# Attention stages given to a scheduler 150 places earlier than the expert steps around them

## The chip, the cores and the metric

The kernel runs on one core of a Trainium2 chip. The metric is the device time of the whole program in microseconds (us). A core has five engines that run their own instruction queues side by side and meet only at semaphores: PE (TensorE, matmuls), DVE (VectorE), ACT (ScalarE), POOL (GpSimd) and SP (SyncE, which here only issues DMAs). Each queue is served in order: an instruction that waits holds everything behind it on its engine.

## The reference

Three layers follow each other, all in fp32. Attention has 4 batches of 8 heads, 576 positions, 64 wide, and each position sees the last 64. The heads are put side by side to 2304 tokens x 512. Expert layer 1 takes 512 to 2048 and back, expert layer 2 takes 512 to 1024 and back.

```python
# attention, q k v: (4, 8, 576, 64)
scores = scale * np.matmul(q, k.transpose(0, 1, 3, 2))
mask = (rel >= 0) & (rel < window)            # rel = query position - key position, window = 64
attn = np.exp(scores - max);  attn = attn / (np.sum(attn) + 1e-09)
x = (attn @ v).transpose(0, 2, 1, 3).reshape(2304, 512)
# layer 1
h = x @ w_in                                  # 512 -> 2048
g = np.where(h >= 1, h, np.where(h <= -1, 0.0, (h + 1) ** 2 / 4))
x = g @ w_out                                 # 2048 -> 512
# layer 2
h = x @ w_in2                                 # 512 -> 1024
solu = h * softmax(h)
x = (layer_norm(solu) * g_ln) @ w_out2        # 1024 -> 512
```

## The kernel before

**Numbers.** Each fp32 factor of an expert matmul is split into a high and a low part, and a product is three matmuls (high-high, high-low, low-high). So each weight tile is converted before its first use: after its DMA (L124 for w_in, L126 for w_out, 512 KB each, five landing buffers `wst`) ACT rescales it (L132), DVE shifts and merges bits (L136, L137), ACT casts the high part (L145), and DVE subtracts to get the low part (L146). `wih`, `wil` are the parts of w_in, `woh`, `wol` those of w_out. There are 16 tiles of each, one per slice f of 128 hidden features.

**Layer 1.** Tokens go in six blocks j of 384, with the 16 slices f inside. A unit of work is one (j, f): 12 matmuls for h (L496), ACT relu and square (L505, L506), DVE min/max (L511, writes `u`), ACT cast (L512), a subtraction for the low part (L516, on POOL in block 0, then on DVE), and, two units later in the program's order, 12 matmuls that add the unit into the output (L527). The weights are loaded and converted during block 0 and stay on chip, so the later blocks need none. The first two slices of block 0 are done in halves of 192 tokens.

**Attention between the units.** Attention goes by groups g (one tile of 192 tokens, two heads), in pairs P of groups from g = 18. A group has loads of q and k (`load_qk`, eight DMAs of 24 or 32 KB, L291, into five `qk` buffers), DVE transposes into `kq` (L325, L326, or L317 for pairs), scores on PE (L352, or L442 for pairs), masked maxima on DVE (L360, L452), exps on ACT (L366, L458), a division on DVE (L377, L378, L382, L386; POOL divides the first three tiles), transposes of the probabilities on PE (L402), copies of these on ACT (L407), probabilities times v on PE (L421, L476), and the result's high part on ACT and low part on DVE (L428, L429, L483, L484), which are `xh` and `xl`, the inputs of layer 1. The function `slots()` is a generator that yields after each stage: four stages a group, eight a pair. The main loop calls `slot(n0)` after the unit's h and before its min/max, and `slot(n1)` after the output matmuls of two units earlier, so two stages fall into each unit (more in the half units).

**What sets the order.** The program runs under a tile framework whose scheduler takes the instructions in the order of their priority, which is the order in which the Python code gives them unless the code says otherwise, and simulates the engines to place each of them in its engine's queue. A stage's loads on SP are ordered the same way as its matmuls.

Of the kernel before, what the change touches and what calls it, by code (L numbers as in the profile page):

```python
# [20 lines left out]
def kernel(  # L21
# [579 lines left out]
    def slots():  # L601
        for g in range(G0 + 1, GB + 1):
            st_s(g)
            yield
            st_v(g - 1)
            st_norm(g)
            yield
            qkt_and_loads(g + 1)
            v_ahead(g)
            yield  # L610
            st_t(g)
            if g == GB:
                st_s(g + 1)
            yield
        st_norm(GB + 1)
        qkt_and_loads(2 * PU)
        yield
        st_v(GB)
        st_t(GB + 1)
        qkt_and_loads(2 * PU + 1)  # L620
        yield
        for P in range(PU, NPP + 1):
            if P == PU:
                st_v(GB + 1)
            else:
                pair_v(P - 1)
            if P % NPR == 0:
                v_ahead(2 * P)
            if P < NPP:
                pair_s(P)  # L630
            yield
            if P < NPP:
                st_norm(P, 0)
                st_norm(P, 1)
            yield
            qkt_and_loads(2 * P + 2)
            yield
            qkt_and_loads(2 * P + 3)
            yield
            yield  # L640
            yield
            if P < NPP:
                st_t(P, 0)
                st_t(P, 1)
            yield
            yield

    stages = slots()

    def slot(n):  # L650
        for _ in range(n):
            next(stages, None)

    TPN = NB // 128
    NK2 = DF2 // 128
# [192 lines left out]
    for n in range(len(seq) + 2):  # L848
# [29 lines left out]
        if n < len(seq):  # L878
            prev = part
            slot(n0)  # L880
            w_conv()
            pins = moe_g2(*part)
# [5 lines left out]
        if n < len(seq):  # L888
            slot(n1)
            w_conv()  # L890
            if j == 0:
                w_load(2)
            w2_step(n, *pins)
            if last and f < 2:
                w2_vals(f)
            if last and f in (2, 3):
                w2_sums(f - 2)
            if last and f >= 2:
                with tc.issue_after(pins[0]):
                    w2_split(f - 2)  # L900
            if last and 2 <= f < 10:
                w2_load(f - 2)
        else:
            w_conv()
# [82 lines left out]
```

## Time and profile before

| | before |
|---|---|
| median of three runs | 707.45 us (706.28, 707.45, 707.75) |
| profiled execution: time | 705.73 us |
| profiled execution: span | 704.0 us |
| mean granted TensorE clock | 0.995 of 2.4 GHz |
| PE busy | 681.7 us, 97% |
| DVE busy | 442.6 us, 63% |
| ACT busy | 411.8 us, 58% |
| POOL busy | 147.6 us, 21% |

The span runs from the first to the last instruction that the profiler saw; the execution's time is 1.7 us more. A busy share is an average over stages that have different limits: in block 0 of layer 1 (about 61 to 141 us) the weights are loaded and converted, in blocks 1 to 5 they are not. An end that is followed by idle time in brackets, as in "[0.76 <-DVE u L511]", says that the engine stood still for 0.76 us before that instruction and that the last thing to arrive was the DVE's result `u` of line 511.

### The profile page before, as it was taken

What the parts mean: (1) busy time and instruction counts of PE and PEld (TensorE: products, weight loads), DVE (VectorE), ACT (ScalarE), POOL (GpSimd) and SP (SyncE); (2) the same over time, 40 slices, a digit from 0 to 9 for tenths busy, and PEclk for the clock granted to TensorE, in tenths of its full rate; (3) what the DMA queues carried; (4) which work ended last, traced back from release to release, by engine and by line L of the source; (5) the groups of instructions that cost most, each with busy time, mean ns of one, the idle gap of its engine ahead of it and who ended that gap; (6) DMA issues with size and microseconds to landing.
All of it is one profiled execution on the core that took longest, in us unless ns stands there. A gap on an engine that the chain in (4) does not pass through costs nothing.

```text
span 704.0 us, 12616 instructions
## 1 busy us (share of the span) xinstructions
PE 681.7 (97%) x4439; PEld 627.7 (89%) x4439; DVE 442.6 (63%) x1179; ACT 411.8 (58%) x1006; POOL 147.6 (21%) x185
## 2 busy tenths in 40 slices
PE   6889999899999999999999999999999999999998
PEld 5689888799999999999999999999987788888887
DVE  4669998556455555454455553642379999988850
ACT  5779777565556655565566565354454746345451
POOL 2313222200001000021112111652272322220000
PEclk9989999999999999999999999999999999999999
DMA  9996798534354524346352211562024465534321
GB/s 188 206 277 179 191 245 215 121 62 108 72 115 106 119 65 77 75 129 125 86 113 67 99 48 43 173 200 92 1 102 123 150 194 166 183 131 141 127 93 46
DMA packets 155543, 88.94 MB, mean 126 GB/s; under 512 B 118616, under 2 KB 141400, under 8 KB 155480
## 3 DMA queue, kind: packets, MB, share of 16 engines
q1 hardware_dynamic: 144040, 64.00, 36.9%
q0 software_dynamic: 8704, 19.41, 8.4%
q10 hardware_dynamic: 2736, 4.72, 1.8%
q8 instruction: 35, 0.57, 0.4%
q14 instruction: 28, 0.23, 0.1%
HBM read 63.97 MB, written 24.12 MB: 125 GB/s over the span
## 4 chain that ended last, share of the span: by engine, by line
PE 74%; DVE 9%; issue 6%; ACT 5%; DMA 4%; POOL 2%; SPq 1%; DVEq 0%; POOLq 0%; ACTq 0%
PE ps_h L496 22%; PE acc L527 22%; PE ps_o L826 13%; PE P L711 8%; DMA wst<-in_moe_w_in_dram 2%; PE ps_x L476 2%; POOL wil L249 2%; PE ps_p L402 2%; PE ps_s L442 2%; PE ps_s L352 1%; ACT p L366 1%; DVE wst L137 1%; DVE gl L516 1%; PE ps_x L421 1%; DVE s L740 1%
## 5 line engine op out<-in xcount | busy, mean ns | idle before, releaser
L511 DVE SCALAR_TENSOR_TENSOR u<-u,ps_h 128x384 f32<-128x384 f32 (+1 forms) x98 | 53.2, 543 | 140.2 <-ACT u L506 139.2
L496 PE MATMUL ps_h<-xh,wih 128*128 128x384 f32 (+1 forms) x392 | 132.1, 338 | 3.1 <-DVE u L511 2.1
L496 PE MATMUL ps_h<-xl,wih 128*128 128x384 f32 (+1 forms) x392 | 131.5, 336 | 0.6 <-DVE xl L429 0.5
L527 PE MATMUL acc<-gl,woh 128*128 128x384 f32 (+1 forms) x392 | 130.5, 334 | 1.5 <-DVE gl L516 1.3
L496 PE MATMUL ps_h<-xh,wil 128*128 128x384 f32 (+1 forms) x392 | 131.4, 335 | 0.0
L527 PE MATMUL acc<-gh,wol 128*128 128x384 f32 (+1 forms) x392 | 129.5, 333 | 0.0
L527 PE MATMUL acc<-gh,woh 128*128 128x384 f32 (+1 forms) x392 | 128.5, 342 | 0.5 <-ACT gh L512 0.5
L505 ACT ACTIVATE u<-ps_h,half 128x384 f32<-128x384 f32 (+1 forms) x98 | 56.0, 572 | 92.7 <-PE ps_h L496 92.5
L512 ACT CAST gh<-u 128x384 fp32r<-128x384 f32 (+1 forms) x98 | 49.7, 507 | 54.6 <-DVE u L511 37.4
L496 PEld LDWEIGHTS ps_h<-xh,wih 128*128 128x128 f32 x392 | 74.3, 190 | 4.9 <-DVE u L511 3.3
L527 PEld LDWEIGHTS acc<-gh,woh 128*128 128x128 f32 x392 | 72.7, 189 | 3.8 <-issue 2.6
L527 PEld LDWEIGHTS acc<-gl,woh 128*128 128x128 f32 x392 | 73.7, 188 | 2.6 <-DVE gl L516 1.7
L516 DVE TENSOR_TENSOR gl<-u,gh 128x384 fp32r<-128x384 f32 x80 | 52.4, 655 | 37.2 <-ACT gh L512 36.7
L496 PEld LDWEIGHTS ps_h<-xl,wih 128*128 128x128 f32 x392 | 74.5, 190 | 1.2 <-DVE xl L429 0.9
L496 PEld LDWEIGHTS ps_h<-xh,wil 128*128 128x128 f32 x392 | 74.6, 190 | 0.1
L527 PEld LDWEIGHTS acc<-gh,wol 128*128 128x128 f32 x392 | 73.6, 188 | 0.1
L711 PE MATMUL P<-wih,x2p 128*128 128x512 f32 x216 | 70.8, 391 | 1.4 <-DVE xo L539 0.9
L826 PE MATMUL ps_o<-woh,wol 128*128 128x512 f32 (+1 forms) x152 | 57.7, 380 | 0.3 <-DVE wol L814 0.3
L826 PE MATMUL ps_o<-woh,woh 128*128 128x512 f32 (+1 forms) x152 | 57.7, 379 | 0.0
L826 PE MATMUL ps_o<-wol,woh 128*128 128x512 f32 (+1 forms) x152 | 57.5, 378 | 0.0
L506 ACT ACTIVATE u<-u 128x384 f32<-128x384 f32 (+1 forms) x98 | 51.1, 522 | 1.9
L711 PEld LDWEIGHTS P<-wih,x2p 128*128 128x128 f32 x216 | 40.4, 188 | 10.4 <-DVE xo L539 1.3
(125 smaller groups left out, 1208.8 us busy)
## 6 DMA issues: line engine op xcount, KB each, us to landing
vw<-in_v_dram SPq DMA_DIRECT2D x32, 256.0 KB, 5.1
wst<-in_moe_w_in_dram SPq DMA_DIRECT2D x16, 512.0 KB, 5.8
wst<-in_moe_w_out_dram SPq DMA_DIRECT2D x16, 512.0 KB, 4.7
lnd<-e SPq DMA_DIRECT2D x16, 512.0 KB, 2.8
lT<-lnd SPq DMA_DIRECT2D x64, 128.0 KB, 2.9
x2d<-xo POOLq DMA_DIRECT2D x24, 192.0 KB, 2.5
out_dram<-o ACTq DMA_DIRECT2D x17, 256.0 KB, 2.0
wst<-in_moe_w_in_dram POOLq DMA_DIRECT2D x8, 512.0 KB, 5.5
```

The source lines that it names most:

```text
L249: nc.gpsimd.tensor_tensor(lo, v_, as_f32(hi), op=ALU.subtract)
L402: nc.tensor.transpose(ps[:, i * 128:i * 128 + 128], p[:, i, :], ident)
L442: nc.tensor.matmul(ps[x][64 * c:64 * c + 64, i * 128 + c0:i * 128 + 128], z[r, KQ + i * 64:KQ + i * 64 + 64], z[r, i * 64 + c0:i * 64 + 12 ...
L496: nc.tensor.matmul(ps, a, bb[:, kc, c], start=(n == 0), stop=(n == 3 * KC - 1))
L505: nc.scalar.activation(u, ps, ACTF.Relu, bias=half, scale=0.5)
L506: nc.scalar.activation(u, u, ACTF.Square)
L511: g = nc.vector.scalar_tensor_tensor(u, u, 1.0, ps, op0=ALU.min, op1=ALU.max)
L512: return nc.scalar.copy(hi, u).ins, g.ins
L516: eng.tensor_tensor(lo, u, as_f32(hi), op=ALU.subtract)
L527: nc.tensor.matmul(acc[j, e][:, c], a, bb, start=(f == 0 and n == 0 and c.start == 0), stop=(f == NF - 1 and n == 2),)
L711: nc.tensor.matmul(ps, l, r, start=(n == 0), stop=(n == 5))
L826: nc.tensor.matmul(ps, a[kk // 4][:, kk % 4, :], b[kk][:, c:c + w], start=(n == 0), stop=(n == 3 * NK2 - 1),)
```

## The change

The stage call is put into a context that gives every instruction of the stage, its DMA issues too, a priority 150 instructions further up. Nothing is added or removed, and every engine has the same instructions as before. After this edit lines from 653 on carry numbers one higher.

```diff
     def slot(n):
         for _ in range(n):
-            next(stages, None)
+            with tc.high_priority(150):
+                next(stages, None)
```

On SP's queue the place is the middle of block 0, where the weights of slice f = 8 follow those of f = 7. `wst` are weights, and each `qk` row is a run of loads for attention groups 13, 14 and so on. Before:

```order
L124 DMA wst<-in_moe_w_in_dram 128x4x256
L126 DMA wst<-in_moe_w_out_dram 128x1024
L291 DMA qk<-in_q_dram 32x6x32 x3
L124 DMA wst<-in_moe_w_in_dram 128x4x256
L291 DMA qk<-in_q_dram 32x6x32
L291 DMA qk<-in_k_dram 32x6x32 x4
L291 DMA qk<-in_q_dram 32x6x32 x4
L126 DMA wst<-in_moe_w_out_dram 128x1024
```

And now, where the first two rows are again the weights of f = 7 and the next `wst` row is w_in of f = 8:

```order
L124 DMA wst<-in_moe_w_in_dram 128x4x256
L126 DMA wst<-in_moe_w_out_dram 128x1024
L291 DMA qk<-in_q_dram 32x6x32 x4
L291 DMA qk<-in_k_dram 32x6x32 x4
L291 DMA qk<-in_q_dram 32x6x32 x4
L291 DMA qk<-in_k_dram 32x6x32 x4
L291 DMA qk<-in_q_dram 32x6x32 x4
L291 DMA qk<-in_k_dram 32x6x32 x4
L124 DMA wst<-in_moe_w_in_dram 128x4x256
L291 DMA qk<-in_q_dram 32x6x32 x4
L291 DMA qk<-in_k_dram 32x8x32 x4
L126 DMA wst<-in_moe_w_out_dram 128x1024
```

The load of w_in for f = 8 stands behind three q/k loads before and behind 24 now, and that of w_out for f = 8 behind 12 before and 32 now. At f = 15, the last slice, w_in stands behind 48 before and 72 now, counted from group 13 on.

On DVE the place is the conversion of the same tile, w_in of f = 8 (`wil_792` is its low part, `wol_788` the low part of w_out for f = 7). Before:

```order
L146 TENSOR_TENSOR wol_788<-wst,woh_787 128x512
L360 ISA p,mx<-ps_s,mask 128x128
...
L325 STREAM_TRANSPOSE kq_125<-qk 64x3x64 x2
L326 STREAM_TRANSPOSE kq_125<-qk 128x192
L511 SCALAR_TENSOR_TENSOR u<-u,ps_h 128x384
L136 TENSOR_SCALAR wst<-wst 128x512
L146 TENSOR_TENSOR wil_792<-wst,wih_791 128x512
```

And now, where the L136 is the shift of w_in for f = 8 itself:

```order
L146 TENSOR_TENSOR wol_788<-wst,woh_787 128x512
L377 TENSOR_SCALAR sm<-sm 128x3
L378 RECIPROCAL rs<-sm 128x3
L511 SCALAR_TENSOR_TENSOR u<-u,ps_h 128x384
L429 TENSOR_TENSOR xl<-ps_x,xh 128x192
L136 TENSOR_SCALAR wst<-wst 128x512
L137 SCALAR_TENSOR_TENSOR wst<-wst 128x512
L511 SCALAR_TENSOR_TENSOR u<-u,ps_h 128x384
...
L325 STREAM_TRANSPOSE kq_124<-qk 64x3x64 x2
L326 STREAM_TRANSPOSE kq_124<-qk 128x192
L146 TENSOR_TENSOR wil_792<-wst,wih_791 128x512
```

The tile's low part stands two units of work ahead of the matmuls that use it before (eight L511 rows precede it in the block), and directly ahead of them now (ten do). From the shift of f = 8 to the low part of w_in for f = 15, DVE's queue now holds, beyond what stood between the low parts of f = 8 and f = 15 before: two L136, one L137, one L146, six maxima with their reads (L360), one L317, two L325, one L326, two L377, one L378, two L382, two L386 and two L429.

On PE the place is a unit of block 1, at the transposes of a pair's probabilities (L402). Before:

```order
L496 MATMUL ps_h<-xh,wih_494 128x384
L496 MATMUL ps_h<-xl,wih_494 128x384
L496 MATMUL ps_h<-xh,wil_495 128x384
L402 MATMUL ps_p<-ident,p 128x128 x6
```

And now:

```order
L527 MATMUL acc_2050<-gh,wol_173 128x384
L496 MATMUL ps_h<-xh,wih_494 128x384
L402 MATMUL ps_p<-ident,p 128x128 x6
L496 MATMUL ps_h<-xl,wih_494 128x384
L496 MATMUL ps_h<-xh,wil_495 128x384
```

The stage follows the first of a unit's 12 matmuls instead of the last: 11 matmuls earlier, and so for each stage of blocks 1 to 4. In block 0 the stages come up to 85 matmuls earlier. When PE reaches the first L442, both orders have the same work behind them, and in the last 1319 rows of PE nothing differs. From the last low part of w_in (f = 15) to the first L442, PE now has 66 matmuls of 384 columns, two groups of L402, one of L352 and two of L421.

## Rows read from the trace of the kernel before

**Rows 1.** The page: busy time of each engine and its share of the span.
```profile
PE 681.7 (97%) x4439; PEld 627.7 (89%) x4439; DVE 442.6 (63%) x1179; ACT 411.8 (58%) x1006; POOL 147.6 (21%) x185
```

**Rows 2.** Windows: stretch, length, busy PE PEld DVE ACT POOL, clock, DMA share, GB/s.
```profile
80.00:100.00 20.00, 18.90 (x119) 17.52 (x119) 19.05 (x43) 15.89 (x36) 5.36 (x5) 1.00 0.85 213
100.00:120.00 20.00, 19.22 (x129) 17.82 (x128) 17.81 (x49) 16.19 (x43) 5.75 (x6) 1.00 0.98 239
120.00:141.00 21.00, 18.78 (x140) 16.76 (x138) 12.76 (x46) 11.73 (x39) 5.95 (x8) 1.00 0.51 113
...
250.00:300.00 50.00, 50.00 (x408) 48.47 (x407) 26.32 (x88) 30.56 (x83) 4.22 (x8) 1.00 0.35 74
```

**Rows 3.** Timeline of PE: start, us, instruction, count, idle before and its releaser.
```profile
82.35 0.33 PE L496 MATMUL ps_h<-xh,wih 128*128 128x384 f32 x1
...
119.70 0.44 PE L496 MATMUL ps_h<-xh,wih 128*128 128x384 f32 x1 [0.76 <-DVE u L511]
...
133.58 0.52 PE L402 MATMUL ps_p<-ident,p 128*128 128x128 f32 x3 [1.37 <-DVE p L386]
...
135.58 0.44 PE L496 MATMUL ps_h<-xh,wih 128*128 128x384 f32 x1 [0.81 <-DVE mx L360]
...
141.45 0.78 PE L442 MATMUL ps_s<-kq 64*64 64x128 f32 x20
```

**Rows 4.** Timeline of SP's DMA issues: start, us for the run, instruction, count.
```profile
63.50 1.30 SPq L291 DMA_DIRECT2D qk<-in_q_dram  x3
64.91 0.39 SPq L124 DMA_DIRECT2D wst<-in_moe_w_in_dram  x1
65.34 0.51 SPq L291 DMA_DIRECT2D qk<-in_q_dram  x1
...
71.28 0.39 SPq L126 DMA_DIRECT2D wst<-in_moe_w_out_dram  x1
...
120.50 1.92 SPq L291 DMA_DIRECT2D qk<-in_k_dram  x4
```

**Rows 5.** The page's DMA issues: count, KB each, median us to landing.
```profile
wst<-in_moe_w_in_dram SPq DMA_DIRECT2D x16, 512.0 KB, 5.8
```

**Rows 6.** Timeline of DVE: low parts of w_in for f = 8 and 15.
```profile
77.12 0.68 DVE L146 TENSOR_TENSOR wil<-wst,wih 128x512 fp32r<-128x512 f32 x1
...
118.53 0.65 DVE L146 TENSOR_TENSOR wil<-wst,wih 128x512 fp32r<-128x512 f32 x1
119.10 0.54 DVE L511 SCALAR_TENSOR_TENSOR u<-u,ps_h 128x384 f32<-128x384 f32 x1
```

**Rows 7.** DVE by line, 77.8 to 119.2 us: busy, mean ns, idle before.
```profile
L137 DVE SCALAR_TENSOR_TENSOR wst<-wst 128x512 uint32<-128x512 uint32 x15 | 11.0, 734 | 0.3 <-ACT wst L132 0.3
L136 DVE TENSOR_SCALAR wst<-wst 128x512 uint32<-128x512 uint32 x14 | 8.2, 584 | 2.9 <-DMA wst<-in_moe_w_in_dram 1.7 <-DMA wst<-in_moe_w_out_dram 1.2
L146 DVE TENSOR_TENSOR wil<-wst,wih 128x512 fp32r<-128x512 f32 x8 | 5.4, 672 | 0.0
L146 DVE TENSOR_TENSOR wol<-wst,woh 128x512 fp32r<-128x512 f32 x7 | 4.8, 682 | 0.8 <-ACT woh L145 0.8
...
L325 DVE STREAM_TRANSPOSE kq<-qk 64x192 f32<-64x192 f32 x6 | 2.2, 368 | 0.1
L360 DVE CUSTOM_DVE_ANT_0 p<-ps_s,mask 128x128 f32<-128x128 f32 (+1 forms) x9 | 1.9, 259 | 0.0
L377 DVE TENSOR_SCALAR sm<-sm 128x3 f32<-128x3 f32 x3 | 1.3, 435 | 0.0
...
L429 DVE TENSOR_TENSOR xl<-ps_x,xh 128x192 fp32r<-128x192 f32 x3 | 1.0, 346 | 0.0
L386 DVE TENSOR_TENSOR p<-p,rs 128x256 f32<-128x256 f32 x2 | 0.8, 418 | 0.0
```

**Rows 8.** Timeline of PE in block 1: two starts twelve matmuls apart.
```profile
161.58 0.33 PE L496 MATMUL ps_h<-xh,wih 128*128 128x384 f32 x1
...
163.66 0.33 PE L527 MATMUL acc<-gh,woh 128*128 128x384 f32 x1
```

## The prediction

> **What bounds the kernel now.** I read the page first. PE is busy for 97% of the span and no other engine for more than 63% [rows 1], so only stretches where PE stands still can give anything back. The windows say which: in block 2 PE is busy for 50.00 of 50.00 us, while in block 0 it is busy for 18.90 and 19.22 of 20 and then 18.78 of 21, together 4.1 us of idle time from 80 to 141 us [rows 2]. The same windows show a second thing: from 80 to 120 us DVE is at 19.05 and 17.81 of 20, nearly as full as PE, and only from 120 us on has it room (12.76 of 21). So block 0 has two engines that are both almost bounds. PE's timeline names the waits: 0.76 us for the min/max of a unit (L511), 1.37 us for a division (L386), 0.81 us for a maximum (L360) [rows 3]; all are for DVE. What fills DVE is in its groups by line: the conversions of weights (L136, L137, L146) are 29.4 of the busy time there, and its own waits are 4.0 us (2.9, 0.3 and 0.8), three quarters of them for weights to land [rows 7]. Behind DVE stands SP, which issues weights and q/k loads in one queue.
>
> **The change, part by part.** Every instruction stays; what counts is what each queue now holds ahead of what. When PE reaches the first L442, at 141.45 us before [rows 3], both orders have done the same work, so I work out when that point comes, and then what follows.
>
> *SP's queue.* The load of w_in for f = 8 was issued at 64.91 us behind three q/k loads that began at 63.50 [rows 4]. Now it stands behind 24 loads. Their buffers come free when group 12 has been transposed, which is when the three began, so I let the 24 start at 63.50 too. The price of one: 1.92 us for four when nothing else runs, 0.48 each; 5.94 us for the nine between 65.34 and 71.28 with weights under way, 0.66 each [rows 4]. The first three took 64.91 less 63.50, 0.47 each. Few weights are under way in the new order, so I take 0.52, near the lower rows: 24 x 0.52 = 12.5 us, an issue at 76.0, and 5.8 us to landing [rows 5]: 81.8 us. With 0.47 it is 80.6, with 0.66 85.1. Weights that came at about 70.7 before come 11 us later.
>
> The DMA queues show this as issue time, not as bytes. The Trainium skill, "Perfetto Trace Analysis", section What "DMA-bound" means, says that a sequencer whose track is solid with DMA slices is itself the bound, and that such slices are descriptor generation; the row of 1.92 us for four loads agrees. Its page "DMA: Bandwidth & Descriptors", section Bandwidth, gives rates by size in which transfers below 64 KB are mostly overhead. By bytes alone, 24 loads of 24 or 32 KB are 0.67 MB, 3 us at the 213 GB/s of that window [rows 2], and the hold would be 9 us shorter; the issue rows speak for the long one.
>
> *DVE's queue.* It is in order, and the shift (L136) of f = 8 stands ahead of a min/max, of maxima and transposes. So DVE waits there from about where its earlier work ends until the tile has landed. What it must then do up to the low part of f = 15: before, the low part of f = 8 ended at 77.80 and that of f = 15 at 119.18 [rows 6], 41.4 us, less the 4.0 of waits [rows 7] 37.4. To that come the extra instructions, by their means [rows 7]: two L136 1.17, one L137 0.73, one L146 0.67, six L360 1.55, four transposes at L325's 0.368 1.47, two L377 0.87, two L429 0.69, four divisions at L386's 0.418 1.67; the reads and the reciprocal I leave out, since the two short divisions are counted as full ones. That is 8.8 us. Neighbours on DVE overlap: the 0.65 us instruction at 118.53 is followed at 119.10, 0.57 later [rows 6], or 88%. So 7.8, and 37.4 + 7.8 = 45.2 us. Waits of DVE within it: at least 0, at most 5, a bit over the 4.0 of before; I take 2, since the weights now come in bunches, with four loads close behind each other and no q/k loads between. Low part of f = 15: 81.8 + 45.2 + 2 = 129.0 us, ten later than before.
>
> *PE behind it.* The last matmuls of block 0 and the first of block 1 follow: 66 of 384 columns, at 2.08 us for twelve [rows 8] 11.4 us, and five short groups at up to the 0.52 us of an L402 [rows 3], 2.6 us. 129.0 + 14.0 = 143.0 us for the first L442, against 141.45: 1.55 us later. The waits of PE that go (0.76, 1.37, 0.81) are inside this comparison, because PE is now behind DVE over the whole stretch and not at single places. PE itself does not starve at f = 8: the attention moved ahead of it, up to 85 matmuls earlier, keeps it busy past the 82.35 us at which that unit began [rows 3], and DVE's hold ends at about the same time. If that cover failed, PE would wait for the conversion after 81.8, about 3 us, but those lie within DVE's stretch and aren't added. Ends: with 0.47 a load and no wait of DVE 81.8 becomes 80.6 and the point 139.8, or -1.65; with 0.66 and 5 us of waits 149.3, or +7.8.
>
> *Blocks 1 to 4.* Each stage comes 11 matmuls earlier, 11 x 0.173 = 1.9 us. PE has no idle time there to win (50.00 of 50.00) [rows 2], so the gain is 0. DVE is at 26.32 of 50 and ACT at 30.56 [rows 2], which covers the moved stages; were it gone, each of the 15 pairs could cost up to the 1.9 us. I take 0. The tail of layer 2 has the same order, 0.
>
> Sum: the profiled execution of 705.73 becomes 707.3. That execution lies 1.7 us below the median of the three runs, so the median goes from 707.45 to 709.0.
>
> **The rivals.**
> *A, the hold costs nothing and PE's waits go: faster.* If DVE needs less than 41.6 us after 81.8 where I have 47.2 (137.4, which is 141.45 less 4.1, less 14.0 and 81.8), or does attention work while it waits, PE decides; the earlier stages then remove the waits, at most the 4.1 us of idle time: 707.45 - 4.1 = 703.4. For it speaks that all three waits are for results of DVE that now stand earlier in its queue. Against it speaks that DVE is in order and at 95% there already [rows 2], and that it gets eight us more of work behind a later start.
> *B, both cancel.* The issue is quicker than I took it (0.47) and DVE waits for 2 to 3 us: 707 to 708, no change to be told. The ends of my sum lie on both sides of it.
> *C, slower by the steady blocks.* In a unit PE now does the scores or transposes behind the first of 12 matmuls. A pair's scores need a PSUM bank that the min/max of an earlier unit must have left, so a score that is 1.9 us earlier may stand at the head of PE's queue with 11 ready matmuls behind it. From the point where the bank's release has less than 1.9 us to spare it decides; a quarter of that, 0.5 us, over 15 pairs is 7.5 us: 715. Against it: DVE is idle for nearly half of that stretch [rows 2], and PE never waits before.
>
> **How the numbers follow.** A change under 0.2%, 1.4 us, can't be told from none. My forecast's case has a chance of 0.52, by itself from 705.8 to 715.2 with its middle at 709.0: 0.36 of it slower, 0.14 within, 0.02 faster. A has 0.25, of which 0.22 is faster and 0.03 within. B has 0.14: 0.12 within, 0.01 on each side. C has 0.09, 0.08 slower and 0.01 within. Together faster 0.25, same 0.30, slower 0.45. The range that should hold 8 in 10 takes in A's time and leaves out C and the forecast's upper end: 703.0 to 713.0.
>
> **What would show it.** In the changed kernel's trace: SP's issues of q/k run without a break for some 12 us from about 63.5, and the load of w_in for f = 8 stands at about 76; DVE idles for several us just before 82, with a wait for that DMA, and then is dense until about 129; the first L442 on PE is at 143. Block 2 stays at 50.00 of 50.00. The forecast is wrong if the load of f = 8 is issued before 70, if the first L442 comes before 140 (then A), or if PE shows waits at L442 or L476 in blocks 1 to 4 (then C).

## The result and the profile after

| | before | changed |
|---|---|---|
| median | 706.74 us (7 runs, 704.38 to 707.75) | 712.25 us (7 runs, 711.12 to 717.34) |
| ratio, 95% interval | | 1.0102 [1.0069, 1.0135] |
| profiled execution, span | 704.0 us | 710.2 us |
| mean granted TensorE clock | 0.995 | 0.986 |

The change makes the kernel slower, as forecast, and its median lies in the range; the loss is 5.5 us between the medians, three and a half times the 1.55 forecast. It comes in two places. In one profiled execution of each kernel, the same matmul starts 3.54 us later at the 23rd unit (the fifth of block 1), still 3.60 later at the last unit of block 5, and 6.27 later from the middle of layer 2 on. So there block 0 costs 3.5 us, blocks 1 to 5 nothing, and layer 2, in which no queue has another order, 2.7.

The page after, whose busy times are within 3 us of those of before [rows 1]:

```profile
PE 682.4 (96%) x4439; PEld 628.8 (89%) x4439; DVE 440.4 (62%) x1179; ACT 414.4 (58%) x1006; POOL 146.3 (21%) x185
```

The windows after (columns as in [rows 2]):

```profile
80.00:100.00 20.00, 18.93 (x127) 16.90 (x126) 17.72 (x57) 16.00 (x44) 3.37 (x3) 1.00 0.91 245
100.00:120.00 20.00, 14.68 (x95) 12.83 (x94) 16.05 (x43) 13.89 (x36) 3.64 (x3) 0.91 0.76 197
120.00:141.00 21.00, 19.54 (x125) 18.47 (x125) 12.32 (x36) 11.65 (x32) 4.47 (x5) 0.92 0.74 164
...
250.00:300.00 50.00, 50.00 (x409) 48.43 (x408) 26.89 (x87) 29.74 (x80) 3.10 (x5) 1.00 0.31 71
...
500.00:600.00 100.00, 96.62 (x445) 82.81 (x444) 80.66 (x173) 50.81 (x95) 35.38 (x41) 0.98 0.38 122
```

Block 2 is as full as before. From 100 to 120 us PE is busy 14.68 of 20 where it was 19.22, and part of that stretch and of the next goes at the lower of the clock's two levels (means 0.91 and 0.92).

SP's issues after (start, us for the run, count), with w_in of f = 8 at 74.44 and that of f = 15 in the last row:

```profile
61.74 1.79 SPq L291 DMA_DIRECT2D qk<-in_q_dram  x4
...
71.80 2.54 SPq L291 DMA_DIRECT2D qk<-in_k_dram  x4
74.44 0.39 SPq L124 DMA_DIRECT2D wst<-in_moe_w_in_dram  x1
74.92 1.90 SPq L291 DMA_DIRECT2D qk<-in_q_dram  x4
76.87 2.07 SPq L291 DMA_DIRECT2D qk<-in_k_dram  x4
79.04 0.40 SPq L126 DMA_DIRECT2D wst<-in_moe_w_out_dram  x1
...
118.49 0.40 SPq L124 DMA_DIRECT2D wst<-in_moe_w_in_dram  x1
```

DVE's timeline after: it stands at the shift of f = 8 until the tile lands, and again at later tiles. In brackets is the wait before the row:

```profile
78.64 0.43 DVE L136 TENSOR_SCALAR wst<-wst 128x512 uint32<-128x512 uint32 x1 [3.39 <-DMA wst<-in_moe_w_in_dram]
...
117.11 0.43 DVE L136 TENSOR_SCALAR wst<-wst 128x512 uint32<-128x512 uint32 x1 [2.80 <-DMA wst<-in_moe_w_in_dram]
```

DVE's waits from 78 to 131 us (us in total, times, longest), against 2.9 us for weights in [rows 7]:

```profile
DVE wst L136 <- DMA wst<-in_moe_w_in_dram: 8.6, 5, 3.4
DVE wst L136 <- DMA wst<-in_moe_w_out_dram: 2.2, 4, 1.3
```

The windows from that shift to the last low part of w_in, and from there to the first L442:

```profile
78.64:130.42 51.78, 43.94 (x281) 39.36 (x280) 42.30 (x120) 37.60 (x97) 8.58 (x9) 0.93 0.86 223
130.42:145.00 14.58, 14.58 (x106) 13.88 (x104) 6.61 (x20) 8.33 (x22) 3.31 (x4) 1.00 0.39 61
```

DVE is busy for 42.30 of the first 51.78 us; in the second stretch PE has no idle time and the full clock.

PE behind it, where the 3.44 us end with matmuls 0.32 us apart (119.69 to 120.01 and on), nearly twice the 0.173 of [rows 8], until after 122.57, and the first L442 answers to the 141.45 of [rows 3]:

```profile
118.24 1.65 PE L527 MATMUL acc<-gh,woh 128*128 128x384 f32 x4 [3.44 <-ACT gh L512]
119.69 0.52 PE L496 MATMUL ps_h<-xh,wil 128*128 128x384 f32 x1
120.01 0.52 PE L496 MATMUL ps_h<-xh,wih 128*128 128x384 f32 x1
...
129.68 0.45 PE L496 MATMUL ps_h<-xh,wih 128*128 128x384 f32 x1 [1.46 <-ACT wih L145]
...
145.00 0.89 PE L442 MATMUL ps_s<-kq 64*64 64x128 f32 x24
```

In layer 2, at the product P1 that opens the second pair, PE after:

```profile
528.71 0.51 PE L712 MATMUL P<-wih,x2p 128*128 128x512 f32 x1 [3.38 <-DVE stat L741]
529.05 0.40 PE L712 MATMUL P<-wil,x2p 128*128 128x512 f32 x1
529.28 0.93 PE L712 MATMUL P<-wih,x2p 128*128 128x512 f32 x2
530.00 0.63 PE L712 MATMUL P<-wil,x2p 128*128 128x512 f32 x1
530.43 1.06 PE L712 MATMUL P<-wih,x2p 128*128 128x512 f32 x2
```

And before, where P1 had run without a wait and only the next product stood, for a copy of an accumulator:

```profile
524.03 0.50 PE L711 MATMUL P<-wih,x2p 128*128 128x512 f32 x1 [0.92 <-DVE xo L539]
```

L741 (L740 before) reads the product ahead, P3, out of its PSUM bank (PSUM is where matmuls write, and each product has one bank of it). The built programs say why PE waits for it: before, P3 is in bank 3 and P1 in bank 0; after, both are in bank 0. The products up to P3 share a ring of four banks with attention; then the ring is closed, and from P1 of the second pair on a new pool gives out six banks. In every program here without a bank order set by hand, the new pool gives that P1 bank 0, while P3 has bank 3, 0 or 1, by which of attention's stages were moved in blocks 0 to 4. That the ring is permuted because the scheduler hands out the bank that comes free first as it simulates is my reading and is not shown. The order of instructions doesn't show the sharing; the banks do.

### The profile page after: what moved, and what is told of

It is laid out like the page before. It is cut to its first block, busy times and chain, and to the rows that moved or that the text cites. A ratio compares the mean times of both kernels' runs of the same rounds, so it can differ in the third digit from the quotient of the medians.

```text
span 710.2 us, 12608 instructions
## 1 busy us (share of the span) xinstructions
PE 682.4 (96%) x4439; PEld 628.8 (89%) x4439; DVE 440.4 (62%) x1179; ACT 414.4 (58%) x1006; POOL 146.3 (21%) x185
## 4 chain that ended last, share of the span: by engine, by line
PE 77%; DMA 6%; issue 5%; DVE 5%; ACT 3%; POOL 2%; SPq 1%; POOLq 0%; DVEq 0%; ACTq 0%
PE ps_h L496 23%; PE acc L527 22%; PE ps_o L827 14%; PE P L712 11%; DMA wst<-in_moe_w_out_dram 4%; PE ps_x L476 2%; POOL wil L249 2%; PE ps_s L442 2%; PE ps_p L402 2%; ACT p L366 1%; DMA wst<-in_moe_w_in_dram 1%; PE ps_s L352 1%; SPq L291 1%; DVE gl L516 1%; DVE wst L137 1%
## 5 line engine op out<-in xcount | busy, mean ns | idle before, releaser
L496 PE MATMUL ps_h<-xh,wih 128*128 128x384 f32 (+1 forms) x392 | 133.0, 340 | 3.3 <-ACT wih L145 3.2
L496 PE MATMUL ps_h<-xl,wih 128*128 128x384 f32 (+1 forms) x392 | 134.6, 344 | 0.7 <-DVE xl L429 0.5
L496 PE MATMUL ps_h<-xh,wil 128*128 128x384 f32 (+1 forms) x392 | 131.9, 337 | 0.3 <-DVE wil L146 0.2
L511 DVE SCALAR_TENSOR_TENSOR u<-u,ps_h 128x384 f32<-128x384 f32 (+1 forms) x98 | 53.2, 544 | 125.1 <-ACT u L506 122.8
L527 PE MATMUL acc<-gh,woh 128*128 128x384 f32 (+1 forms) x392 | 123.9, 337 | 3.4 <-ACT gh L512 3.4
L496 PEld LDWEIGHTS ps_h<-xh,wih 128*128 128x128 f32 x392 | 74.8, 191 | 4.8 <-ACT wih L145 4.0
L496 PEld LDWEIGHTS ps_h<-xl,wih 128*128 128x128 f32 x392 | 74.9, 191 | 4.1 <-issue 2.4
L496 PEld LDWEIGHTS ps_h<-xh,wil 128*128 128x128 f32 x392 | 75.0, 191 | 0.7 <-DVE wil L146 0.7
```

The source lines that it names most:

```text
L496: nc.tensor.matmul(ps, a, bb[:, kc, c], start=(n == 0), stop=(n == 3 * KC - 1))
L511: g = nc.vector.scalar_tensor_tensor(u, u, 1.0, ps, op0=ALU.min, op1=ALU.max)
L527: nc.tensor.matmul(acc[j, e][:, c], a, bb, start=(f == 0 and n == 0 and c.start == 0), stop=(f == NF - 1 and n == 2),)
```

## The experiments

Two causes are proposed: weights behind q/k loads on SP (block 0), called the queue theory below, and the shared bank (layer 2), the bank theory. Rivals: DVE's moved attention work, stages of blocks 1 to 4, and scatter. For every run the table has the ratio to the kernel before; how much later than in the profile of before the 23rd unit starts (one execution each); the further step in layer 2 (from P3 of the first pair to the 35th product); and the banks of P3 and P1. That profile of before is one of its quickest executions (the 29 runs of before beside e5 to e8 took 704.28 to 711.81 us), so a few us at the 23rd unit are what the unchanged program shows too: e14 has 4.90, and up to there it is the program of before.

| run | ratio | 23rd unit, us | step in layer 2, us | P3, P1 |
|---|---|---|---|---|
| changed | 1.0102 [1.0069, 1.0135] | 3.54 | 2.67 | 0, 0 |
| e1 loads back | 1.0048 [1.0010, 1.0085] | 2.68 | 2.67 | 0, 0 |
| e2 loads only | 1.0098 [1.0067, 1.0130] | 9.76 | 0.01 | 3, 0 |
| e4 later only | 1.0043 [1.0014, 1.0072] | 3.73 | 2.66 | 0, 0 |
| e5 changed, other bank | 1.0050 [1.0023, 1.0078] | 6.64 | 0.63 | 0, 3 |
| e6 changed, same bank | 1.0093 [1.0063, 1.0122] | 2.80 | 3.85 | 0, 0 |
| e7 before, other bank | 0.9992 [0.9971, 1.0014] | 2.86 | -0.01 | 3, 0 |
| e8 before, same bank | 1.0035 [1.0005, 1.0065] | 0.29 | 2.65 | 3, 3 |
| e9 block 0 only | 1.0055 [1.0029, 1.0081] | 5.95 | 0.03 | 1, 0 |
| e10 later only | 1.0096 [1.0058, 1.0135] | 6.12 | 2.47 | 0, 0 |
| e11 priority 300 | 1.0170 [1.0112, 1.0228] | 10.22 | 3.69 | 0, 0 |
| e12 early units | 1.0035 [1.0010, 1.0061] | 6.83 | 0.04 | 3, 0 |
| e13 turn of blocks | 1.0046 [1.0020, 1.0071] | 3.83 | 0.01 | 3, 0 |
| e14 after the turn | 1.0083 [1.0052, 1.0114] | 4.90 | 2.70 | 0, 0 |
| e15 both repairs | 1.0064 [1.0027, 1.0100] | 2.16 | 0.00 | 0, 3 |
| e16 null | 0.9994 [0.9971, 1.0016] | 0.43 | -0.01 | 3, 0 |
| e17 later, other bank | 1.0017 [0.9998, 1.0036] | 1.51 | 0.90 | 0, 3 |
| e18 after the turn, other bank | 0.9985 [0.9962, 1.0007] | 4.31 | 0.73 | 0, 3 |

**The bank (e5 to e8).** In both kernels the order in which layer 2's products take their six banks is set by hand:

```diff
+    bank = [3, 1, 2, 4, 5, 0]        # e5, e8;  [0, 1, 2, 4, 5, 3] in e6, e7
     def p_bank(name):
         if ps2:
-            return ps2[0].tile([128, 512], F32, tag="p", bufs=6, name=name)
+            bank.append(bank.pop(0))
+            return ps2[0].tile([128, 512], F32, tag=f"p{bank[-1]}", bufs=1, name=name)
...
+    for z in range(6):
+        ps2[0].tile([128, 512], F32, tag=f"p{z}", bufs=1, name="p_first")
```

The last two lines make six unused tiles, which tie each tag to its bank.

> The changed kernel, in which only the order of layer 2's six product banks is set by hand to 3, 1, 2, 4, 5, 0: P1 of the next pair takes bank 3, while P3 sits in bank 0. Bank theory: the wait of 3.4 us before that P1 goes, and the 2.7 us lost in layer 2 with it; 3.5 us of block 0 stay: 709 to 710, or 0.9 less if the old wait for L539 goes too. Rival (the loss is one of phase: all of layer 2 starts at another moment): 712 as the changed kernel.

> Control for e5: the changed kernel with the bank order 0, 1, 2, 4, 5, 3, so P1 takes bank 0, where P3 is. Bank theory: the wait of about 3.4 us stays, 711.5 to 713. Rival (any hand-set order helps or hurts by itself): the same time as e5.

> The kernel before with the bank order 0, 1, 2, 4, 5, 3: P3 is in bank 3, P1 takes bank 0, P6 bank 1 instead of 5. Bank theory: no loss; the old wait of 0.9 us for L539 before P6 goes: 705.5 to 707.

> The kernel before with the bank order 3, 1, 2, 4, 5, 0: now P1 takes bank 3, where P3 is. Bank theory: PE waits about 3.4 us before that P1 and the kernel before loses the 2.7 us without any change of attention's priority: 709 to 710. Rival (phase): 706 to 707.

The step follows the bank, not the kernel: 3.85 and 0.63 us in the changed kernel, 2.65 and 0.00 in the one before, and in all eighteen rows 2.47 us or more where the banks are equal and 0.90 or less where not. e8 has no moved stage, and PE stands there as in the changed kernel:

```profile
525.41 0.50 PE L714 MATMUL P<-wih,x2p 128*128 128x512 f32 x1 [3.37 <-DVE stat L743]
```

So it is shown that equal banks make the wait and the step in layer 2. In time e8 costs 0.35%, 2.5 us. Five pairs of runs differ by the bank order alone, and equal banks are 0.43% slower in e8 against e7 and e6 against e5, 0.79% in e10 against e17, 0.98% in e14 against e18, but 0.16% quicker in e1 against e15; with intervals of 0.2 to 0.4% either way the times agree with the step of the traces on the whole and can't measure it. e7's hope, the old 0.9 us wait, was a miss: that wait is gone, but its step is 0.00, since PE waits longer for an input further on (`x2p` of L693: 0.21 and 0.84 us, where it was 0.51).

**The loads (e1, e2, e11).** e1 takes the loads back, e2 gives the 150 to the loads alone (there with `150`, and the plain call in `slot`), e11 has 300 for 150. The scheduler simulates anew each time, so neither e1 nor e2 has exactly the queue that was meant. Counted on SP from w_out of f = 7, w_in of f = 8, 9 and 15 has 3, 14 and 48 q/k loads ahead of it before, 24, 32 and 72 in the changed kernel, 3, 12 and 55 in e1, and 7, 24 and 68 in e2. The edit of e1:

```diff
-            load_qk(m + 4)
+            with tc.high_priority(-150):
+                load_qk(m + 4)
...
-            load_v(t + 1)
+            with tc.high_priority(-150):
+                load_v(t + 1)
```

> Stages keep the 150, but the loads of q, k and v inside them are taken back to their old place, so SP's queue is about that of before. Queue theory (block 0 loses 3.5 us because weights stand behind 24 q/k loads on SP): no loss in block 0; the 19th unit's h matmuls start within 1 us of 135.6 or up to 2.5 earlier, DVE waits for weights between 78 and 131 us fall from 10.8 us to about 4. Here the last product of layer 2's first pair (P3) and the next pair's first (P1) share PSUM bank 0, as in the changed kernel, so by the bank theory (2.7 us lost in layer 2 by that) the span is about 706 to 707 and the time 707.5 to 709.5. Rival (the attention work moved ahead on DVE delays the conversions): block 0 stays 3.5 us late, the time is 712.

> Only the loads of q, k and v get the 150, the stages' matmuls and vector work don't. Queue theory: block 0 loses 2 to 4 us, the first L442 at 143.5 to 145.5 instead of 141.45. P3 is in bank 3 and P1 in bank 0, as in the kernel before, so by the bank theory layer 2 loses nothing: 709 to 710.5. Rival (the moved vector work): block 0 as before, 706 to 707.

> The changed kernel with 300 in place of 150: on SP 40 q/k loads stand between w_out of f = 7 and w_in of f = 8 instead of 24 (before 3). Queue theory: 16 more loads at about 0.5 us hold f = 8 by 8 us more, and some of them wait for transposes: block 0 loses 8 to 20 us, P3 and P1 share bank 0, 2.7 more: 717 to 730. Rival (the loss in block 0 is scatter between executions, 0 to 3 us): 710 to 713.

e2 and e11 go the way of the queue theory. e2 is above its numbers: 0.98%, 6.9 us, where 2 to 4 were expected, without a step in layer 2. It doesn't repeat the hold at f = 8 (out at 70.34 us behind seven loads); it is late at the later weights, and w_in of f = 15 goes out at 121.97. In e11, with two timed runs only, the load of w_in for f = 8 goes out at 84.91 us behind 40 q/k loads from 61.63 on and three of v (74.44 with 24), the 11th unit starts 12.63 us late, and from the 24th on it is some 12.3. SP's issues in e11:

```profile
61.63 1.79 SPq L291 DMA_DIRECT2D qk<-in_q_dram  x4
...
80.78 1.92 SPq L291 DMA_DIRECT2D qk<-in_k_dram  x4
...
84.91 1.15 SPq L124 DMA_DIRECT2D wst<-in_moe_w_in_dram  x1
```

e1 is a half miss. The last low part of w_in ends at 119.08 us there, as before (119.18, [rows 6]), against 130.42 in the changed kernel. All runs divide that way: it ends at 129.66 to 134.44 us in the six kernels in which block 0's loads have the 150 (changed, e2, e3, e5, e6, e9), at 140.95 in e11, and at 117.18 to 122.77 in the thirteen others, among them e1, e12 and e15, whose attention work is moved without its loads. So it is the place of the loads, and not DVE's moved attention work, that makes the conversions late. PE's time doesn't follow as simply. In e1 it was 3.18 us ahead at the 17th unit, but its wait for `u` ends at 119.60, where that of before ends at 119.70 [rows 3]: DVE had stood for weights ahead of that `u`. PE's clock is then at the lower level for part of the time (120 to 141 us: mean 0.85), and the 23rd unit is 2.68 us late. DVE's shift and PE's wait in e1:

```profile
116.67 0.43 DVE L136 TENSOR_SCALAR wst<-wst 128x512 uint32<-128x512 uint32 x1 [2.77 <-DMA wst<-in_moe_w_out_dram]
```

```profile
119.60 0.69 PE L496 MATMUL ps_h<-xh,wih 128*128 128x384 f32 x1 [3.84 <-DVE u L511]
```

**Which part of the program (e3, e4, e9, e10, e13, e14, e17, e18).** The context is given by a unit's number, in e9 so, in e10 and e17 with `>= 18`, in e14 and e18 with `>= 22`, in e13 from 18 to 20:

```diff
         for _ in range(n):
-            next(stages, None)
+            if step[0] < 18:
+                with tc.high_priority(150):
+                    next(stages, None)
+            else:
+                next(stages, None)
```

> As e3 was meant: the 150 for stages called in block 0, and from block 1 on the stages are called without any context, since in e3 the context with offset 0 made stage and unit share their priorities and PE alternate between them (15 us a block). Order on SP and DVE in block 0 is that of the changed kernel; P3 is in bank 1, P1 in bank 0. Queue theory: block 0 loses what e2 and the changed kernel lose there, 3 to 6 us; bank theory: 0 in layer 2: 710 to 713, and PE has no 3.4 us wait before P1. If the tail's loss were tied to block 0's lateness, 2.7 more and that wait.

> The 150 only from block 1 on, stages of block 0 called plainly, so that every queue of block 0 stands as before; P3 and P1 share bank 0. Bank theory: no loss up to layer 2 beyond the scatter of block 0, 0 in blocks 1 to 4, 2.7 in layer 2 with the 3.4 us wait: a ratio of 1.003 to 1.005, 709 to 711. Rival (the moved stages of blocks 1 to 4 cost or win something themselves): a step between the 23rd unit and layer 2.

> The 150 only for the stages of the first three units of block 1 (units 19 to 21), where e10 lost 3.2 us in its profile with the clock at half for 6 us; banks as in the kernel before (P3 in 3, P1 in 0). If the moved stages at the turn of blocks cost the 4 us that e10 has beyond the bank: 710 to 712 against 707.9. If that was scatter of one set of runs: 706.5 to 708.5.

> The 150 only from the 23rd unit on, past the turn; P3 and P1 share bank 0. Bank theory: 2.5 to 2.7 us and no more, a ratio of 1.003 to 1.005, about 710.5. If e10's other 4 us come from the steady stages: 714 to 715.5 again.

> e10 with the bank order 3, 1, 2, 4, 5, 0, so that P1 no longer shares P3's bank: stages from block 1 on at 150, nothing else moved. If the bank is all that blocks 1 to 4 bring: ratio 0.998 to 1.002. If the stages moved from the turn of blocks on cost about 4 us, as e10 beyond its bank: 1.004 to 1.007.

> e14 with that bank order: stages from the 23rd unit on at 150. Up to there the program is that of before. Bank theory: 0.998 to 1.002. If the steady stages cost 3 us of their own, as e14 beyond its bank: 1.003 to 1.006, and the timed runs' clock is lower than before's.

e9 is as expected, 0.55% or 3.9 us with the banks apart: block 0's own share. e10 and e14 were far above expectation, 0.96% and 0.83%. But their profiles show no step between the 23rd unit and layer 2 (6.12 to 6.18 and 4.90 to 4.93 us), and with the banks apart and more runs the same moves cost 0.17% [-0.02, 0.36] (e17) and -0.15% [-0.38, 0.07] (e18): the steady blocks cost nothing that these runs can tell. Their excess over the bank's 0.35% isn't explained by an order. They had four runs each, and scatter of block 0 is a guess, since all four of e10 lie between 714.40 and 715.75 us. e13's 0.46% stands against e17's 0.17%, which moves the same stages and more; whether the turn costs 1 or 2 us stays open. e13's profile is no sign of it: it loses 1.54 us from the 19th to the 23rd unit, and e14 and e18, still the program of before there, lose 1.47 and 1.53.

e3 and e4 gave the offset as `150 if ... else 0`. 

> The 150 only for stages called in block 0 (the first 18 units). P3 and P1 share bank 0. Queue and bank theory together: 3.5 us in block 0, 0 in blocks 1 to 4, 2.7 in layer 2: 712 to 713. If the tail's loss came from the moved stages of blocks 1 to 4: 709.5 to 710.5.

> The 150 only for stages called from block 1 on. P3 and P1 share bank 0. Queue and bank theory: block 0 as before, 0 in blocks 1 to 4, 2.7 in layer 2: 709 to 710. If the steady blocks cost something of their own (15 pairs), more than that; if the bank doesn't matter: 706 to 707.

e4 agrees with the bank alone, though its block 0 isn't quite that of before: with the offset 0 PE's order differs from the 12th unit on. e3 is a miss by its construction (1.16, in its profile 24 to 32 us in each of blocks 1 to 4, not the 15 that e9's expectation says): PE alternates there between a stage and the unit, as I read it because with offset 0 a stage and the code behind it get the same priorities. That is told at the end.

**Repairs and the null (e12, e15, e16).** e15 joins e1 and e5; e12 has e1's loads and `step[0] < 10`; e16 is one unused line.

> The changed kernel with both repairs: loads of q, k, v at the old place on SP (as e1) and bank order 3, 1, 2, 4, 5, 0 (as e5), all stages at 150. Queue and bank theory: the loss is gone, 707 to 709, ratio 0.999 to 1.002. If the moved stages themselves cost something: 710 or more. If the lead of 3 us that e1 had at the eighth unit survives: 705.

> A try at beating both: the 150 only for the stages of the first ten units, their loads at the old place, the rest plain; P3 in bank 3, P1 in bank 0. In e1 PE was 3.3 us ahead at the seventh unit by that. Queue theory: nothing is lost on SP; if the lead survives the second half of block 0, 704 to 706; if conversions on DVE and weights decide there, it is given back: 706 to 708. Rival (moved vector work costs): 709 or more.

> The kernel before with one unused Python line: the same program. It measures the scatter that the others are to be read by: ratio 0.998 to 1.002, and a block 0 that ends 0 to 5 us later than in the profile of before.

e16 is as expected. e15 and e12 are misses: 0.64% and 0.35% slower, where the loads' way was to be free. In both PE's early lead is gone by the 19th unit, as in e1: in e15 the last low part of w_in ends at 120.08, and PE waits 2.63 us twice, each time for L511. So moved stages without moved loads cost block 0 too, in these two runs about 2.5 to 4.5 us, in e1 0.9 beyond the bank, although e1 and e15 have the same block 0: so wide is the scatter. The loads alone cost 6.9 us (e2), both together 3.9 (e9). The parts don't add. No version here is measurably faster than the kernel before.

## Why the prediction was right in its sign and wrong in its size

Two steps failed. The tail of layer 2 was put at 0 and lost 2.67 us, and the first L442 came 3.55 us late instead of 1.55, because DVE's waits for weights were put too low and PE's work behind them too short.

- *SP's queue*: right. The 24 loads began at 61.74 instead of 63.50, at 0.53 us each to 74.44 where 76.0 was forecast, and the tile was there at 78.64 instead of 81.8. The issue rows, not the bytes, gave the time: SP shows no gap over 0.1 us in those 12.7 us. The Trainium skill, "Perfetto Trace Analysis", section What "DMA-bound" means, says of a sequencer's track that is solid with DMA slices that it is the bound; this trace agrees.
- *DVE's queue*: the end was nearly right, 130.42 for the last low part of w_in against 129.0, but by luck. The step "Waits of DVE within it: at least 0, at most 5 [...] I take 2" failed: DVE waited 7.4 us for weights after f = 8 had landed (the 10.8 less the first 3.39) and stood still for 9.5 in all (51.78 less 42.30). I had followed one hold, at f = 8, and taken the one bunch of four weights behind it for the rule. After the bunch q/k loads stand between the weights again: w_in of f = 10 has 32 q/k loads ahead of it and f = 15 has 72, so f = 15 went out at 118.49, 13.4 us later than before, and DVE stood again and again where it was to be dense. Two errors hid this one: the tile came 3.2 us earlier, and the work took 42.30 us, not 45.2.
- *PE behind it*: 145.00 for the first L442, not 143.0. Of the 2.0 us, 1.4 are DVE's later end, and 0.6 are this term: from the last low part PE took 14.58 us for 14.0. It had no idle time and the full clock there, so the term was short of work: 68 matmuls of 384 columns were still to start, 11.8 us at 0.173, and the short groups took the other 2.8. The clock's lower level lies ahead of this stretch. At f = 8 PE didn't starve, as forecast; the 3.44 us come later, within DVE's stretch.
- *Blocks 1 to 4 cost 0*: right (3.54 to 3.60 in the profile; e18).
- *"The tail of layer 2 has the same order, 0"*: this step failed outright, by 2.67 us. The order is the same and the banks are not; e8 makes the loss without the change.
- *Rivals*: A and B are out. C had the right kind of wait, a PSUM bank that an earlier reader must leave, but in blocks 1 to 4, where it doesn't occur.

3.55 us to the first L442 and 2.67 in layer 2 give 6.2, the 6.2 between the spans of two single executions. In time, block 0 (e9, 0.55%) and the bank (e8, 0.35%) make 0.90%, inside the changed kernel's [0.69, 1.35]. That within block 0 the loads do it is shown for the lateness of the conversions (117 to 123 us, or some 130 and more), and e2 and e11 agree in time. How much of the 3.9 us would be left without them isn't settled, since e1, e12 and e15, with the conversions in time, lose in block 0 too: so for the time of block 0 the cause is in part argued.

## What to carry to other kernels

A priority on a stage moves its DMA issues as well; count what stands ahead of every later load on the issuing queue, not only of the first. An order that is unchanged in a late stage doesn't make that stage unchanged: compare the buffers and PSUM banks that the two programs were given, where one pool takes over from another above all. And take three or more runs of an unchanged copy before reading a few microseconds off one profile.

## What the hardware showed that was not expected

PE's waits can cost more than their length. After the 3.44 us matmuls of 384 columns start 0.32 us apart for some 3 us, at the lower of the clock's two levels, where they take 0.173 at the upper. In layer 2 the products behind P1's wait show the same: 0.43 us from one start to the next at 530.00, 0.23 at 529.05.

The length of a wait doesn't settle it. Up to the 22nd unit e7 and e18 are both the program of before, and both have the waits of 1.37 and 0.81 us of [rows 3] near the turn to block 1. Behind them the clock stays up in e7 and falls in e18 (PE's rows, then the window from 139 us on with the clock behind the busy times):

```profile
138.42 0.44 PE L496 MATMUL ps_h<-xh,wih 128*128 128x384 f32 x1 [0.81 <-DVE mx L360]
138.70 0.33 PE L496 MATMUL ps_h<-xl,wih 128*128 128x384 f32 x1
...
139.00:142.00 3.00, 3.00 (x29) 2.68 (x28) 1.66 (x5) 1.35 (x6) 0.91 (x2) 1.00 1.03 210
```

```profile
138.36 0.44 PE L496 MATMUL ps_h<-xh,wih 128*128 128x384 f32 x1 [0.81 <-DVE mx L360]
...
138.91 0.52 PE L496 MATMUL ps_h<-xh,wil 128*128 128x384 f32 x1
...
139.00:142.00 3.00, 3.00 (x11) 2.80 (x9) 1.37 (x4) 0.18 (x2) 0.98 (x2) 0.50 1.10 216
```

e14 falls like e18; before, e8 and e16 stay up with the same two waits. From the 19th to the 23rd unit e14 and e18 lose 1.47 and 1.53 us and e7 and e16 0.02, so a part of the scatter of one program is its clock. In e15 PE waits 2.63 us twice: behind the first wait the clock is at 0.50 (92 to 95 us), behind the second it is at 1.00 (121 to 124).

Small matmuls woven into large ones are dear. In e3 PE alternates two L442 of 64 x 64 with one L496 of 128 x 128 (start, us, count):

```profile
200.74 0.44 PE L496 MATMUL ps_h<-xl,wih 128*128 128x384 f32 x1
201.11 0.43 PE L442 MATMUL ps_s<-kq 64*64 64x128 f32 x2
201.47 0.44 PE L496 MATMUL ps_h<-xh,wil 128*128 128x384 f32 x1
```

Such a round takes 0.73 us (200.74 to 201.47). In one piece 24 L442 take 0.89 us (at 145.00 in the changed kernel), 0.037 each, and an L496 0.173, which would make 0.25 for the round, at the same full clock. Alternating the two shapes costs the other half microsecond, about a quarter for each of the two changes in a round. What makes it isn't shown. The weight load of a round's L496 starts together with its matmul, at 200.74:

```profile
200.74 0.19 PEld L496 LDWEIGHTS ps_h<-xl,wih 128*128 128x128 f32 x1 [0.17 <-issue]
```

The Trainium skill, "TensorEngine Tiling (Array Packing)", section Key Properties, says that a change of the tiling mode drains TensorE. The time of these rounds agrees with that; no row shows the drain itself.
